# Moving the exps of two chunks ahead of copies, and eight score columns from TensorE to VectorE, in the last head of a streaming attention kernel

## Chip, cores, metric

One core of a Trainium2 chip. The metric is the device time of one execution in microseconds (us), here the median of several executions; a profile was taken of one execution in each run of a kernel. Engines in the profile: PE = TensorE (PEld its weight loads), DVE = VectorE, ACT = ScalarE, POOL = GpSimd, SP = SyncE, which issues the loads.

## The reference

One decode step of a pre-norm transformer block. What matters here is the attention over a long cache:

```python
q = (layernorm(x) @ wq) split into 32 heads of 192          # one query row
scores = einsum("bhqd,bhkd->bhqk", q, k_cache) * 192 ** -0.5   # 32768 keys a head
p = softmax(scores)
o = einsum("bhqk,bhkd->bhqd", p, v_cache)
h = x + o @ wo
out = h + relu(layernorm(h) @ w1) @ w2                       # feed-forward, 640 -> 1536 -> 640
```

Both caches together are 805 MB of bfloat16, each byte used once.

## The kernel before

The kernel streams heads through SBUF. Each head is cut into chunks of 32 columns of 128 keys. For part of a chunk's columns (`jp`), PE transposes the keys into PSUM, ScalarE copies them out, PE multiplies by the query, and ScalarE takes the exp (`exp_pe`). For the other `jd = jc - jp` columns VectorE does a multiply and a reduction, and ScalarE takes that exp too (`exp_dve`). Then PE multiplies all columns by the values. The last head has its own table of chunks, ten of them, the last four small:

```python
JPS = (20, 16)                      # PE columns of even and odd chunks
ends = [(c // 2, (c % 2) * J, J, JPS[c % 2]) for c in range(NC - 2)]      # NC = 8, J = 32
ends += [(NL - 1, 0, 20, 12), (NL - 1, 20, 20, 12), (NL, 0, 16, 8), (NL + 1, 0, 8, 8)]
```

ScalarE's program in a head (engines run in program order; waits are on semaphores):

```python
for c in range(n):
    ...
    copies(g, h, c)                 # waits for the transposes of chunk c
    if h == LAST:
        if c > 5:
            exp_dve(g, h, c - 2)    # waits for VectorE's scores
        if c > 0:
            exp_pe(g, h, c - 1)     # waits for PE's scores
        if 0 < c < 5:
            exp_dve(g, h, c - 1)
if h == LAST:
    exp_dve(g, h, n - 2)
exp_pe(g, h, n - 1)
exp_dve(g, h, n - 1)
```

PE's program in the last head, its beginning and its end. All PE scores go to one PSUM tile, so the scores of chunk c wait for the exp of chunk c - 1:

```python
transposes(g, h, 0)
transposes(g, h, 1)
scores_pe(g, h, 0)
values(g, h, 0)             # waits for both exps of chunk 0
scores_pe(g, h, 1)
transposes(g, h, 2)
o_turn(g, h - 1)            # turns the output of the head before; VectorE waits for it
values(g, h, 1)
...
scores_pe(g, h, 8)
scores_pe(g, h, 9)
for c in (5, 6, 7):
    values(g, h, c)
den_mm(g, h)                # sum of the softmax denominators
values(g, h, 8)
values(g, h, 9)
```

The softmax here doesn't subtract the row's maximum and nothing guards it: scores larger than these inputs give would overflow.

## Time and profile before

| | value |
|---|---|
| time, three runs before the prediction | 1922.64 us median (1921.29 to 1923.37) |
| span of the profiled execution | 1923.4 us |
| time, 38 runs of this kernel in the whole study | 1923.2 us mean (1920.7 to 1925.8) |

The prediction shows the page and the chain. Besides those, from the page, the busy time of each engine:

```profile
PE 1557.5 (81%) x15908; PEld 1087.0 (57%) x15908; DVE 1560.1 (81%) x732; ACT 938.8 (49%) x2000; POOL 1.0 (0%) x6
```

PE and VectorE are equally busy. Two lines of the timeline of the last head (start, duration, engine, line, operation, and in brackets the idle time before it with what ended it):

```profile
1872.23 0.22 DVE L723 TENSOR_SCALAR oT<-mm,odd 128x3 bf16<-128x3 f32 x1 [1.37 <-PE mm L364]
1903.46 0.45 PE L364 MATMUL sp<-qm,kT 128*128 128x2 bf16 x12 [0.36 <-ACT pB L613]
```

The first: VectorE waits 1.37 us for PE's turned output. The second is the scores of chunk 9, from which PE runs without a gap to its last value product.

### The profile page before, as it was taken

The page shows a single profiled execution, that of the slowest core. Times are in us where ns is not written, and L with a number is a line of the kernel's source. Part 1 is how long each engine was busy: PE and PEld are TensorE (multiplying, and loading weights), DVE is VectorE, ACT ScalarE, POOL GpSimd, SP SyncE. Part 2 cuts the span into 40 slices and gives each one's busy share as a digit, 9 for nine tenths or more (in the row PEclk, how much of TensorE's full clock was granted, in tenths as well). Part 3 has the DMA queues.
Part 4 walks back from the last instruction along what each step waited for, and adds up shares of the span by engine and source line. Part 5 has one row for each costly group of instructions (what it writes and reads, how often), then busy time and mean ns, then how long its engine had stood idle before and what let it go on. Part 6 is the DMA issues. An engine that isn't in the chain of part 4 may idle for free.

```text
span 1923.4 us, 36133 instructions
## 1 busy us (share of the span) xinstructions
PE 1557.5 (81%) x15908; PEld 1087.0 (57%) x15908; DVE 1560.1 (81%) x732; ACT 938.8 (49%) x2000; POOL 1.0 (0%) x6
## 2 busy tenths in 40 slices
PE   7878887887888788878878877878787878788788
PEld 7555555655565555555655555555555556555555
DVE  2797787987878978789887879878798787897886
ACT  2455454554544554545544535545455445455444
POOL 0000000000000000000000000000000000000000
PEclk9788998888988889988899888899888898888888
DMA  9999999999999999999999999999999999999997
GB/s 411 423 437 430 429 436 431 438 427 436 433 438 427 436 433 430 439 430 433 437 429 431 440 427 437 435 430 436 433 430 433 439 427 437 430 434 437 430 430 300
DMA packets 29634, 825.29 MB, mean 429 GB/s; under 512 B 3115, under 2 KB 4652, under 8 KB 8108
## 3 DMA queue, kind: packets, MB, share of 16 engines
q1 hardware_dynamic: 29610, 824.98, 99.5%
q8 instruction: 15, 0.25, 0.0%
q14 instruction: 7, 0.06, 0.0%
q10 hardware_dynamic: 2, 0.00, 0.0%
HBM read 824.97 MB, written 0.00 MB: 429 GB/s over the span
## 4 chain that ended last, share of the span: by engine, by line
DVE 39%; DMA 38%; PE 16%; ACT 6%; issue 1%; DVEq 0%; POOLq 0%; SPq 0%
DMA kt<-in_A_k_cache_dram 34%; DVE sc L701 18%; DVE pr L698 18%; PE o_ps L364 8%; PE tp L383 6%; ACT kT L607 5%; DMA va<-in_A_v_cache_dram 4%; PE sp L364 1%; DVE o_pair L713 1%; ACT pA L622 1%; DVE oT L723 0%; DMA kt<-in_A_wq_dram 0%; DVE rec L706 0%; DVE rec L707 0%; DVE odd L719 0%
## 5 line engine op out<-in xcount | busy, mean ns | idle before, releaser
L698 DVE TENSOR_TENSOR pr<-kt,qb 128x2304 f32<-128x2304 bf16 (+2 forms) x257 | 755.9, 2941 | 316.1 <-POOLq L325 288.1
L607 ACT COPY kT<-tp 128x1024 bf16<-128x1024 bf16 (+1 forms) x899 | 814.4, 1016 | 286.8 <-PE tp L383 286.8
L383 PE MATMUL tp<-ident_f,kt 128*128 128x128 f32 x3459 | 588.5, 330 | 238.4 <-POOLq L346 160.9
L701 DVE TENSOR_REDUCE sc<-pr 128x12 f32<-128x2304 f32 (+2 forms) x257 | 755.3, 2939 | 8.9
L383 PEld LDWEIGHTS tp<-ident_f,kt 128*128 128x128 f32 x3459 | 482.5, 170 | 290.4 <-POOLq L346 166.2
L364 PE MATMUL o_ps<-va,pB 128*2 128x384 bf16 x1152 | 222.6, 341 | 62.7 <-POOLq L346 62.7
L364 PEld LDWEIGHTS sp<-qm,kT 128*128 128x128 bf16 x6918 | 197.7, 98 | 83.4 <-issue 43.4
L364 PE MATMUL o_ps<-vb,pB 128*2 128x384 bf16 x1154 | 217.4, 335 | 27.2 <-ACT pA L622 25.0
L364 PE MATMUL sp<-qm,kT 128*128 128x2 bf16 x6918 | 214.7, 164 | 25.7 <-ACT pB L613 24.5
L622 ACT ACTIVATE pA<-sc 128x12 bf16<-128x12 f32 (+2 forms) x257 | 58.3, 227 | 338.8 <-DVEq L65 338.8
L613 ACT ACTIVATE pB<-sp 128x20 bf16<-128x20 f32 (+2 forms) x258 | 52.1, 202 | 307.2 <-PE sp L364 307.2
L364 PEld LDWEIGHTS o_ps<-va,pB 128*2 128x2 bf16 x1152 | 94.3, 86 | 159.2 <-POOLq L346 70.2
L364 PE MATMUL o_ps<-va,pA 128*2 128x384 bf16 x896 | 172.8, 334 | 0.0
L364 PE MATMUL o_ps<-vb,pA 128*2 128x384 bf16 x894 | 167.7, 328 | 0.0
L364 PEld LDWEIGHTS o_ps<-vb,pB 128*2 128x2 bf16 x1154 | 90.9, 85 | 129.1 <-ACT pA L622 30.8
L364 PEld LDWEIGHTS o_ps<-va,pA 128*2 128x2 bf16 x896 | 77.6, 87 | 76.9 <-issue 10.8
L364 PEld LDWEIGHTS o_ps<-vb,pA 128*2 128x2 bf16 x894 | 75.5, 84 | 71.3 <-issue 1.9
L613 ACT ACTIVATION_READ_ACCUMULATOR pB<-sp 128x1 f32 x258 | 55.1, 213 | 0.0
L622 ACT ACTIVATION_READ_ACCUMULATOR pA<-sc 128x1 f32 x257 | 53.1, 207 | 0.0
L364 PE MATMUL o_ps<-xn_ln,kt 128*96 128x1 bf16 (+1 forms) x316 | 22.3, 208 | 2.6 <-DMA kt<-in_A_wq_dram 2.6
L364 PEld LDWEIGHTS o_ps<-xn_ln,kt 128*96 128x96 bf16 (+1 forms) x316 | 22.2, 176 | 2.6 <-issue 2.6
L713 DVE TENSOR_SCALAR o_pair<-o_ps,rec 2x384 bf16<-2x384 f32 x32 | 19.4, 605 | 2.8 <-PE o_ps L364 1.7
(69 smaller groups left out, 187.3 us busy)
## 6 DMA issues: line engine op xcount, KB each, us to landing
kt<-in_A_k_cache_dram SPq DMA_DIRECT2D x62, 6144.0 KB, 26.8
vb<-in_A_v_cache_dram SPq DMA_DIRECT2D x63, 3072.0 KB, 20.8
va<-in_A_v_cache_dram SPq DMA_DIRECT2D x31, 6144.0 KB, 26.8
kt<-in_A_k_cache_dram SPq DMA_DIRECT2D x3, 3072.0 KB, 21.0
wo_s<-in_A_wo_dram SPq DMA_DIRECT2D x16, 480.0 KB, 19.0
kt<-in_A_wq_dram SPq DMA_DIRECT2D x4, 1536.0 KB, 10.8
va<-in_A_v_cache_dram SPq DMA_DIRECT2D x1, 3072.0 KB, 23.1
va<-in_A_v_cache_dram SPq DMA_DIRECT2D x2, 1536.0 KB, 33.9
```

Source lines behind the costliest of these rows:

```text
L364: return lambda: pe.matmul(o, lhsT=w, rhs=r, **kw)
L383: calls.append(lambda b=b, o=o: pe.transpose(out=dst[:, b, :], in_=src[:, o:o + 2 * P].bitcast(f32), identity=ident_f[:]))
L607: g.do(lambda: act.copy(out=kT[c % 2][:, b0:b0 + nb, :], in_=src[:, 0:nb, :].bitcast(bf16)), "act_pe", ("cp", h, c, k))
L613: g.do(lambda: act.activation(out=pB[c % NB][:, 0:jp], in_=sp[:, 0:jp], func=F.Exp, scale=SCALE, accum_out=dsums[:, 2 * c + 1:2 * c + 2]), ...
L622: g.do(lambda: act.activation(out=pA[c % NB][:, 0:jd], in_=sc[c % NC][:, 0:jd], func=F.Exp, scale=SCALE, accum_out=dsums[:, 2 * c:2 * c + ...
L698: g.chain(lambda: dve.tensor_tensor(out=pr[:, 0:j1 - j0, :], in0=src[:, (off + j0) * Dh:(off + j1) * Dh].rearrange("p (j d) -> p j d", d=D ...
L701: g.chain(lambda: dve.reduce_sum(out=sc[c % NC][:, j0:j1], in_=pr[:, 0:j1 - j0, :], axis=X), "dve")
L713: g.do(lambda: dve.tensor_scalar_mul(out=o_pair[:, :, 1, :], in0=o_ps[0:2, 0:2 * Dh].rearrange("q (i d) -> q i d", i=2), scalar1=rec[0:2, ...
```

## The change

The intent: chunk 0's and chunk 1's exps come straight behind their scores, so that PE need not wait for them through the next chunk's copies; chunks 0 and 2 give VectorE 16 columns instead of 12, which spares PE and ScalarE work.

```diff
-    ends = [(c // 2, (c % 2) * J, J, JPS[c % 2]) for c in range(NC - 2)]
+    ends = [(c // 2, (c % 2) * J, J, JPS[c % 2] if c > 3 else 16) for c in range(NC - 2)]
@@ ScalarE, last head
                 if c > 5:
                     exp_dve(g, h, c - 2)
-                if c > 0:
+                if c > 2:
                     exp_pe(g, h, c - 1)
-                if 0 < c < 5:
+                if c < 2:
+                    exp_pe(g, h, c)
+                    exp_dve(g, h, c)
+                elif 2 < c < 5:
                     exp_dve(g, h, c - 1)
```

## The prediction

> **What bounds the kernel now.** I read the page first, then the chain of waits of the last head in order of time, then the last 70 us engine by engine, then stretches of 5 us for the clock and the DMA.
>
> ```profile
> DMA  9999999999999999999999999999999999999997
> q1 hardware_dynamic: 29610, 824.98, 99.5%
> ```
>
> The DMA row (mean busy share of the 16 DMA engines, in 40 slices) and the queue's share say that the kernel streams its caches for the whole span; no change to the last head touches the first 31. Only what lies between the end of the stream and the end of the program can be won. Two stretches (the columns after the widths are busy time of PE, PEld, DVE, ACT, POOL; then clock, DMA share, GB/s) show where the stream ends:
>
> ```profile
> 1905.00:1910.00 5.00, 5.00 (x32) 2.55 (x30) 0.00 (x0) 0.52 (x1) 0.00 (x0) 1.00 1.00 373
> 1910.00:1915.00 5.00, 3.71 (x38) 2.33 (x38) 1.60 (x10) 0.00 (x0) 0.00 (x0) 0.93 0.08 29
> ```
>
> It ends near 1911 us, and the span is 1923.4 us. The chain in the last head (start, duration, what):
>
> ```profile
> 1861.12 0.90 PE sp L364 x30
> 1862.02 2.24 issue
> 1864.26 5.28 PE o_ps L364 x16
> 1869.54 0.72 PE sp L364 x24
> 1870.26 0.51 PE tp L383 x4
> 1870.77 0.02 issue
> 1870.79 3.55 ACT kT L607 x4
> 1874.34 0.17 ACT pB L613 x2
> 1874.51 0.20 ACT pA L622 x2
> 1874.71 0.04 issue
> 1874.75 2.76 PE o_ps L364 x16
> ...
> 1903.46 0.45 PE sp L364 x12
> 1903.91 5.94 PE o_ps L364 x36
> ```
>
> sp are scores, tp transposes, o_ps the products with the values, kT the copies out of PSUM. From 1874.75 on, PE has hardly a gap until its last value product at 1912.2, so the end is PE's backlog, and the backlog begins in the two holes at the top: PE idle 2.24 us before chunk 0's values (the "issue" is really the wait for both exps of chunk 0), which then run cold in 5.28 us instead of 2.76 as for chunk 1; then 2.56 us idle (1872.20 to 1874.75) before chunk 1's values. Why the exps are late, in ScalarE's order of time:
>
> ```profile
> 1857.51 6.30 ACT L607 COPY kT<-tp 128x1024 bf16<-128x1024 bf16 x7 [7.54 <-PE tp L383]
> 1863.63 0.27 ACT L613 ACTIVATE pB<-sp 128x20 bf16<-128x20 f32 x1
> 1870.79 3.55 ACT L607 COPY kT<-tp 128x1024 bf16<-128x1024 bf16 x4 [6.63 <-PE tp L383]
> 1874.19 0.23 ACT L613 ACTIVATE pB<-sp 128x16 bf16<-128x16 f32 x1
> ```
>
> Chunk 0's scores are done at 1862.0, but its exp stands behind the copies of chunk 1 as well (7 copies of 0.90 us). Chunk 1's scores are done at 1870.3, but its exp stands behind chunk 2's copies. Beside this VectorE runs without a gap from chunk 3 to chunk 8 (three lines of it):
>
> ```profile
> 1872.65 3.36 DVE L698 TENSOR_TENSOR pr<-kt,qb 128x3072 f32<-128x3072 bf16 x1
> 1897.21 1.75 DVE L701 TENSOR_REDUCE sc<-pr 128x8 f32<-128x1536 f32 x1
> 1900.97 1.75 DVE L701 TENSOR_REDUCE sc<-pr 128x8 f32<-128x1536 f32 x1
> ```
>
> The second is the end of chunk 7 (1898.96), the third of chunk 8 (1902.72). They will matter below.
>
> **What the Trainium skill says.** "TensorE: Matmul & The Clock Gate", Part 1: the array drops to half its clock after about a 3.4 us window without enough activity and needs such a window of work to come back. The trace agrees: the granted clock is 0.51 from 1865 to 1870, and value matmuls begin there at 336 ns instead of 179. "Perfetto Trace Analysis", Tensor Engine Instruction: ScalarE and VectorE are strict FIFO; so an exp that is ready cannot pass a copy that waits, as seen above. "VectorE: DVE Perf Modes", the TRN2 errata section, gives (N+151)/0.96 ns for a 1x tensor_tensor: 3.357 us for 3072, 2.557 for 2304; the trace has 3.36 and 2.56. "ScalarE: Activation LUTs", What ACT_TABLE_LOAD costs, gives 186 ns + 0.833 ns per element for an immediate-operand ACTIVATE, about 0.2 us for 16 columns; the trace has 0.18 to 0.28.
>
> **The change part by part.**
>
> Columns. Chunks 0 and 2 go from 20 PE columns and 12 on VectorE to 16 and 16. VectorE: per chunk (3.36 - 2.56) + (3.35 - 2.55) = 1.6 us more. PE: per chunk 3 transposes (12 take 1.53 us, 15 take 1.83: 0.3 us) and 6 score matmuls (0.90 to 0.75) less. ScalarE: one copy of 0.8 to 0.9 us less. Value products: 16 matmuls as before.
>
> VectorE's first 1.6 us are mostly hidden. Chunk 0 starts at 1850.86 when its keys land and now ends at 1857.60, told at about 1857.7; PE's denominator is ready at 1857.04, where VectorE waited 1.03 us. So chunk 1 is 0.68 us late, 1858.66, and ends at 1865.38. Chunk 2's keys land at 1865.3 to 1865.4 (issue 1837.57 plus 27.7 us), so it starts at 1865.5, only 0.1 late, ends at 1872.24 instead of 1870.56; the turned output of the previous head, for which VectorE waited 1.37 us until 1872.23, is by then ready. Chunk 3 starts at about 1873.03 instead of 1872.65. Of 3.2 us added, 0.4 remain.
>
> Order. Chunk 0: three copies end at 1857.51 + 2.7 = 1860.2; scores 1860.25 to 1861.0; exps 1861.05 and 1861.23 (VectorE's scores lie ready); values start at about 1861.6 instead of 1864.26, and with about 0.8 us of idle before them I expect them warm: to 1864.4 instead of 1869.5. Copies of chunk 1 run beside them, 1861.45 to 1864.2; its scores 1864.4 to 1865.1, its exps 1865.15 and 1865.5 (after VectorE's 1865.38). Transposes of chunk 2 from 1865.4, when the keys land, to 1867.0; the turn 0.3; values of chunk 1 at about 1867.2 instead of 1874.75: **7.5 us earlier at this point**.
>
> What remains of it downstream, step by step: values of chunk 2 wait for a load that lands at 1879.8 (1856.70 + 23.1): 1879.9 instead of 1886.6, gain 6.7, after a long low stretch, so probably cold, which the slack bears. The second exp of chunk 3 now waits for VectorE (1873.03 + 6.7 = 1879.8). Transposes of chunk 6 wait for keys that land at 1884.4 (1857.07 + 27.3) or for PE: about 1885 instead of 1891.6. The second exp of chunk 5 waits for VectorE, 1891.95; scores of chunk 7 at about 1892.6 instead of 1898.7, gain 6.1. The second exp of chunk 7 stands ahead of the first of chunk 8 and waits for VectorE's chunk 7: 1898.96 + 0.38 = 1899.34, exp 1899.45, first exp of chunk 8 0.20 later, scores of chunk 9 another 0.32 later (both gaps as before: 1903.14 to 1903.46), 1899.95 instead of 1903.46. **Gain 3.5 us**: VectorE has become the limit. Behind it the order is unchanged: values of chunks 5 to 7, denominator, chunks 8 and 9. Their loads land by 1902, VectorE's chunk 8 by 1903.1, all before PE asks. The value loads are released earlier, but the queue was never dry, so they and the weights land as before: first weights at about 1906.6 (used at 1911.7), the last near 1911 (used at 1913.8 instead of 1917.32). So the 3.5 us reach the end: 1922.64 - 3.5 = 1919.1.
>
> **The rivals.**
> 1. The gain of 6 to 7 us survives to the end (1916). For it: PE has no gap from 1874.75 to the end. Against: VectorE's row, which cannot be passed: chunk 7 ends at 1898.96 with no gap behind it.
> 2. PE, now waiting about 2.7 us before the scores of chunk 9, goes cold just before its 8.4 us of last value products; one window at half clock costs about 3.4/2 = 1.7 us, so 1920.8. For it: 5.2 us between value products with 2.8 us of idle mostly left them cold in earlier heads (1842.38: 318 ns). Against: of some twenty such stretches of 3.3 to 4.8 us, only two were cold; here it is 3.6 us. I give it 1 in 5.
> 3. The stream bounds the end and nothing is won (1922.6). For it: DMA is at 9 tenths to the last slice. Against: it ends near 1911, six us before the product that needs its last bytes starts.
> 4. The added VectorE columns and the in-order exps stall ScalarE so long that the new order loses, up to 1924. Against: its copies gain 5 us before the first such wait that did not exist before.
>
> **Range and chances.** The centre is 1919.2: 3.5 us of gain, with a little taken off for rival 2. Before ranges over 2.1 us in three runs, and my chain may be off by 1 us either way: 1917.3 to 1921.6. Two per cent are 38 us, out of reach when only the last 60 us change: faster 0.003, within 0.994, slower 0.003.
>
> **What would show it right or wrong.** First values of the last head at about 10.8 us after the keys of chunk 0 land (13.4 before), at 180 ns each; values of chunk 1 7.5 us earlier; VectorE's chunk 3 about 0.4 us later; a new hole in PE before the scores of chunk 9, ended by ScalarE's exp, which itself waited for VectorE; DMA's end unmoved near 1911. The step most likely to fail is the last: if PE has no hole there, it was PE and not VectorE that set the end; if the hole is there and the products after it take over 300 ns, it is rival 2. It is wrong altogether if the stream ends at another time, or an earlier head differs.

## The result, and the profile after

| | before | after |
|---|---|---|
| timed on the same chip, 4 runs each | 1922.83 us (1921.29 to 1923.37) | 1922.93 us (1920.84 to 1923.39) |
| ratio of means | | 1.000, 95% interval 0.9982 to 1.0017 |
| span of the profiled execution | 1923.4 us | 1920.8 us |

All ratios here are the mean time of one kernel's runs over that of the other's of the same rounds, so not quite the ratio of the medians quoted. No gain of 3.5 us is seen, and the time lies outside the predicted range. The traces differ by 2.6 us in span all the same (0.6 us of it because the last head began earlier), so I read where the predicted gain appeared and where it went. PE in the changed kernel's last head:

```profile
1861.15 1.46 PE L364 MATMUL o_ps<-vb,pB 128*2 128x384 bf16 x8 [0.61 <-issue]
...
1899.43 0.45 PE L364 MATMUL sp<-qm,kT 128*128 128x2 bf16 x12 [1.29 <-ACT pB L613]
1899.81 2.17 PE L364 MATMUL o_ps<-va,pB 128*2 128x384 bf16 x8
1901.77 2.48 PE L364 MATMUL o_ps<-va,pA 128*2 128x384 bf16 x8
```

The first part worked as intended: the values of chunk 0 start at 1861.15 (1864.26 before) and run warm, at 182 ns each (a value product is called warm here at about 180 ns, with a granted clock of 1.00, and cold at 300 ns and more, with a clock near 0.5); those of chunk 1 start at 1866.45 (1874.75). The last three lines are the new hole: PE waits 1.29 us for ScalarE's exp before the scores of chunk 9, and chunk 5's value products behind it are cold (2.48 us for 8, where 8 take 1.46 warm). The hole is shorter than the 2.7 us of the prediction because chunk 4's value products ahead of it were cold too (16 in 4.4 us, where warm ones take 2.8); where they were warm, in the second trace (run 2 below), it is 2.98 us. The chain of waits shows who set the hole:

```profile
1895.28 1.77 DVE pr L701
...
1897.07 1.76 DVE sc L704
...
1898.92 0.30 ACT pA L622 x2
1899.22 0.16 ACT pB L613 x2
...
1899.43 0.45 PE sp L364 x12
1899.88 7.62 PE o_ps L364 x36
```

The chain now runs through VectorE's chunk 7 (pr, sc), its exp (pA), the exp of chunk 8 behind it in ScalarE's order (pB), and the scores of chunk 9 (sp). The 36 value products of chunks 5 to 7 take 7.62 us in the chain; the same 36 took 5.94 us before. VectorE ahead of this:

```profile
1868.33 3.35 DVE L704 TENSOR_REDUCE sc<-pr 128x16 f32<-128x3072 f32 x1
...
1872.10 0.22 DVE L726 TENSOR_SCALAR oT<-mm,odd 128x3 bf16<-128x3 f32 x1
...
1872.51 3.36 DVE L701 TENSOR_TENSOR pr<-kt,qb 128x3072 f32<-128x3072 bf16 x1
```

It waits for nothing between chunk 2 and chunk 3 any more: the wait of 1.37 us for the turned output is gone, and a longer chunk 2 stands in its place. Clock and stream (columns as in the prediction):

```profile
1900.00:1905.00 5.00, 5.00 (x22) 2.20 (x21) 2.56 (x2) 1.74 (x5) 0.00 (x0) 0.66 1.03 413
1910.00:1915.00 5.00, 3.45 (x98) 3.11 (x99) 1.84 (x11) 0.56 (x2) 0.00 (x0) 0.91 0.05 17
```

The granted clock is 0.66 of full speed where it was 1.00 before; the stream ends before 1911 as it did.

To compare traces whose last head begins at different times I count from VectorE's first instruction of the last head, which starts when its first keys land. The table is worked out from the timelines; "scores 9" is the start of PE's scores of chunk 9, "to den" the time from there to the denominator's matmul, "head" the time to the end of the span.

| trace | start | VectorE chunk 3 | scores 9 | to den | head |
|---|---|---|---|---|---|
| before, 1st | 1850.86 | 21.79 | 52.60 | 6.32 | 72.54 |
| before, 2nd | 1850.67 | 20.53 | 52.02 | 6.33 | 71.63 |
| before, 3rd | 1850.28 | 20.59 | 49.33 | 6.33 | 69.02 |
| before, 4th | 1849.89 | 20.54 | 52.21 | 6.32 | 72.21 |
| after, 1st | 1850.23 | 22.28 | 49.20 | 8.00 | 70.57 |
| after, 2nd | 1849.87 | 22.28 | 49.20 | 8.00 | 70.53 |
| after, 3rd | 1851.88 | 22.28 | 49.19 | 6.33 | 68.82 |
| order only | 1850.77 | 20.53 | 47.68 | 6.33 | 67.33 |
| columns only | 1849.94 | 22.28 | 49.77 | 6.32 | 69.46 |
| order, 16 columns in chunk 0 | 1850.17 | 20.68 | 47.60 | 6.32 | 67.23 |
| order, 16 columns in chunk 2 | 1850.59 | 22.15 | 49.40 | 6.32 | 69.11 |
| after + idle matmuls | 1850.05 | 22.28 | 49.20 | 6.32 | 69.05 |
| after + values 5 moved | 1850.92 | 22.28 | 50.27 | 3.72 | 67.48 |
| best parts | 1851.62 | 20.69 | 48.17 | 3.72 | 65.78 |

The table hides one difference ahead of the last head. PE's denominator of the head before starts 5.74 us after "start" in the first trace of the kernel before and 4.06 to 4.10 us in its other three; in the changed kernel's three it is 5.75, 4.06 and 4.06. Where it is late, a group of 16 value products of the head before (at 1842.38 in the first trace) had run cold, in 4.4 us instead of 2.8. So both first traces begin the last head with PE 1.7 us behind.

(In the two last rows with moved values, chunk 5's value products stand ahead of the scores of chunk 9, so "to den" holds only those of chunks 6 and 7.)

### The profile page after: what moved, and what is told of

Same layout as the page of the kernel before. It is cut to its first block, busy times and chain, and to the rows that moved or that the text cites. A ratio compares the mean times of both kernels' runs of the same rounds, so it can differ in the third digit from the quotient of the medians.

```text
span 1920.8 us, 36095 instructions
## 1 busy us (share of the span) xinstructions
PE 1558.5 (81%) x15890; PEld 1090.5 (57%) x15890; DVE 1563.3 (81%) x732; ACT 938.0 (49%) x1998; POOL 1.0 (0%) x6
## 4 chain that ended last, share of the span: by engine, by line
DVE 42%; DMA 37%; PE 14%; ACT 5%; issue 1%; DVEq 0%; POOLq 0%; SPq 0%
DMA kt<-in_A_k_cache_dram 35%; DVE sc L704 20%; DVE pr L701 20%; PE o_ps L364 7%; PE tp L383 6%; ACT kT L607 4%; DMA va<-in_A_v_cache_dram 2%; DVE o_pair L716 1%; PE sp L364 1%; ACT pA L622 0%; DVE oT L726 0%; DMA kt<-in_A_wq_dram 0%; DVE rec L709 0%; DVE rec L710 0%; DVE odd L722 0%
## 5 line engine op out<-in xcount | busy, mean ns | idle before, releaser
L701 DVE TENSOR_TENSOR pr<-kt,qb 128x3072 f32<-128x3072 bf16 (+2 forms) x257 | 757.5, 2948 | 314.9 <-POOLq L325 286.8
L704 DVE TENSOR_REDUCE sc<-pr 128x16 f32<-128x3072 f32 (+2 forms) x257 | 756.9, 2945 | 8.9
L622 ACT ACTIVATE pA<-sc 128x16 bf16<-128x16 f32 (+2 forms) x257 | 58.0, 226 | 349.7 <-DVEq L65 349.7
L613 ACT ACTIVATE pB<-sp 128x16 bf16<-128x16 f32 (+2 forms) x258 | 51.8, 201 | 306.0 <-PE sp L364 306.0
## 6 DMA issues: line engine op xcount, KB each, us to landing
kt<-in_A_wq_dram SPq DMA_DIRECT2D x4, 1536.0 KB, 10.9
```

Of the source, the lines that this page charges most:

```text
L613: g.do(lambda: act.activation(out=pB[c % NB][:, 0:jp], in_=sp[:, 0:jp], func=F.Exp, scale=SCALE, accum_out=dsums[:, 2 * c + 1:2 * c + 2]), ...
L622: g.do(lambda: act.activation(out=pA[c % NB][:, 0:jd], in_=sc[c % NC][:, 0:jd], func=F.Exp, scale=SCALE, accum_out=dsums[:, 2 * c:2 * c + ...
L701: g.chain(lambda: dve.tensor_tensor(out=pr[:, 0:j1 - j0, :], in0=src[:, (off + j0) * Dh:(off + j1) * Dh].rearrange("p (j d) -> p j d", d=D ...
L704: g.chain(lambda: dve.reduce_sum(out=sc[c % NC][:, j0:j1], in_=pr[:, 0:j1 - j0, :], axis=X), "dve")
```

## The experiments

All kernels gave the reference's result, and all timed runs of 1 to 9 are fast runs; runs 10 to 12 are one execution each, which has no state of its own ("unknown" in the record). Three calls of four kernels each; the medians of the kernel before in them were 1923.45, 1924.12 and 1923.52 us, over 9 runs each. The cause first put forward (theory A) was: order frees PE, then VectorE sets the scores of chunk 9, and the clock behind the hole gives back 1.7 us. Rivals: the loads before the last head vary (B); the eight columns eat what the order wins (C).

**1. The kernel before, again** (no edit; 5 runs).

> The kernel before, unchanged, for a second trace and the spread. In its first trace the last head took 72.7 us from the landing of its first keys (1850.7) to the end (1923.4), and that execution (1925.2 us) was slower than all four timed ones (1921.3 to 1923.4). Theory A (the clock's phase: the last head of the kernel before is often shorter than in its first trace, where chunk 0's and chunk 2's values were cold): this trace's last head takes 70.5 to 71.5 us, with chunk 0's value matmuls or chunk 2's at about 180 ns. Theory B (the stream of the heads before varies, the last head does not): the last head takes 72.7 us again and its start is earlier or later. Time ratio 1.000 either way.

Measured: 1922.38 us median (1920.73 to 1924.74), ratio 0.9993 (0.9979 to 1.0006). The last head took 71.6 us, just beyond the upper end of theory A's range, with both named value groups cold again, wholly or in part; its traced execution (1924.10 us) was again slower than the mean. VectorE's chunk 3 started at 20.5 us, without the 1.37 us wait of the first trace. Neither theory is settled by it; it does show that the first trace was not typical in that wait: PE came to the last head 1.7 us later there (see under the table).

**2. The changed kernel, again** (no edit; 5 runs).

> The changed kernel, unchanged. In its first trace the last head took 70.7 us from 1850.1 to 1920.8, with chunk 5's value matmuls cold (16 of them in 4.4 us instead of 2.8) behind a hole of 1.29 us. Theory A: 69.0 to 70.8 us, 1.7 us less where those matmuls are warm. The scores of chunk 9 follow VectorE's chunk 7 by 0.6 us in any case. Time against before: 1.000 plus or minus 0.0008.

Measured: 1922.36 us median (1922.28 to 1922.55), ratio 0.9994 (0.998 to 1.0008). Scores of chunk 9 at 49.20 us, to the hundredth as before, and cold behind the hole again. Chunk 0's value products were cold too this time, after only 0.60 us of idle.

**3. Order only.**

```diff
-... JPS[c % 2] if c > 3 else 16) for c in range(NC - 2)]
+... JPS[c % 2]) for c in range(NC - 2)]
```

> The new places of the exps, with 12 columns on VectorE for chunks 0 and 2 as before. Theory A (VectorE sets the scores of chunk 9): VectorE's chunk 7 ends 0.4 us earlier, so the time is 0 to 0.5 us below the changed kernel's. Rival C (the columns eat what the order wins): at least 2 us below the changed kernel, 0.999 of before or less.

Measured: 1919.86 us median (1918.70 to 1921.10), ratio 0.9981 (0.9967 to 0.9994): 2.5 us below the changed kernel. Theory A's number for it fell and rival C's was met. VectorE and PE in its trace:

```profile
1865.33 2.56 DVE L701 TENSOR_TENSOR pr<-kt,qb 128x2304 f32<-128x2304 bf16 x1 [1.60 <-POOLq L325]
1871.30 3.36 DVE L701 TENSOR_TENSOR pr<-kt,qb 128x3072 f32<-128x3072 bf16 x1
1898.45 0.45 PE L364 MATMUL sp<-qm,kT 128*128 128x2 bf16 x12 [0.36 <-ACT pB L613]
1898.83 1.46 PE L364 MATMUL o_ps<-va,pB 128*2 128x384 bf16 x8
```

VectorE waits 1.60 us for chunk 2's keys (first line), starts chunk 3 at 20.53 us instead of 22.28, and PE's hole before the scores of chunk 9 is 0.36 us, with warm products behind it. So the columns cost VectorE 1.75 us by chunk 3, where the prediction had counted 0.4 from the first trace of the kernel before. The theory for the runs that follow: chunk 0's extra columns lie in VectorE's wait for keys and are free, chunk 2's are what costs (tested by 7 and 8); the clock's part is tested by 4 and 5.

**4. The values of chunk 5 ahead of the scores of chunk 9, in the changed kernel.**

```diff
         scores_pe(g, h, 8)
+        values(g, h, 5)
         scores_pe(g, h, 9)
-        for c in (5, 6, 7):
+        for c in (6, 7):
             values(g, h, c)
```

> The changed kernel, with the values of chunk 5 in front of the scores of chunk 9, so that PE works in the hole while ScalarE waits for VectorE. Theory A: the hole goes, and PE's last value product ends about 3 us earlier than in the changed kernel's first trace (1906.9 instead of 1909.9, if its last head starts at the same time), so 1.3 to 3 us below the changed kernel, ratio to before about 0.9988. Rival (the stream of loads bounds the end): its last landing near 1911 leaves no gain over 0.5 us.

Measured: 1919.42 us median (1919.14 to 1920.23), ratio 0.9979 (0.9965 to 0.9992), 2.9 us below the changed kernel. The hole is gone; the last value group starts at 55.6 us instead of 58.8. The stream did not bind here.

**5. Twelve idle matmuls in the hole, in the changed kernel.**

```diff
         scores_pe(g, h, 8)
+        for _ in range(12):
+            g.do(mmul(mm[0:2, 208:496], ident_b[:, 0:2], wide[:, 0:288], start=True, stop=True, skip_group_check=True))
         scores_pe(g, h, 9)
```

> The changed kernel with 12 idle matmuls (2x288, constant operands, result never read) in front of the scores of chunk 9, to keep the array's clock up in the hole; no useful work is moved. If the cold clock gives back 1.7 us (rival 2 of the prediction): scores of chunk 9 still 49.2 us after VectorE's start of the last head, but 6.3 us from there to the denominator instead of 8.0, last head 68.9 instead of 70.5 us, time 1.7 us below the changed kernel. If the cold clock does not matter: 70.5 us and the changed kernel's time.

Measured: 1921.17 us median (1920.83 to 1922.25), ratio 0.9986 (0.9973 to 1.0). In the trace:

```profile
1896.19 1.63 PE L364 MATMUL mm<-wide 128*2 128x288 bf16 x12
1899.25 0.45 PE L364 MATMUL sp<-qm,kT 128*128 128x2 bf16 x12 [1.42 <-ACT pB L615]
1899.63 1.46 PE L364 MATMUL o_ps<-va,pB 128*2 128x384 bf16 x8
```

Scores of chunk 9 at 49.20 us as predicted, warm products behind, 6.32 us to the denominator, head 69.05 us. The size of the clock's loss is thus measured: 8.00 against 6.32, 1.7 us. But the changed kernel's third trace (run 12) was warm without the idle matmuls, so one warm trace does not show that they caused it, and the two ratios' intervals overlap. What is shown is the loss when it is cold.

**6. Columns only.**

```diff
-    ends = [(c // 2, (c % 2) * J, J, JPS[c % 2]) for c in range(NC - 2)]
+    ends = [(c // 2, (c % 2) * J, J, JPS[c % 2] if c > 3 else 16) for c in range(NC - 2)]
```

> 16 columns on VectorE for chunks 0 and 2, exps in their old places. Theory (columns load VectorE with 1.6 us, order frees PE): values of chunk 1 start about 1 us earlier than in the kernel before, since a copy, six transposes and twelve score matmuls are gone, PE stays the limit, and the last head takes 70.5 to 71.8 us: 0.5 to 1.5 us below the kernel before. Rival (the columns alone are harmful): at or above the kernel before.

Measured: 1921.24 us median (1920.74 to 1923.29), ratio 0.9988 (0.9974 to 1.0001), so perhaps below the kernel before, not clear of noise. In the trace the scores of chunk 9 stand at 49.77 us with a hole of 0.36 us, the head at 69.46 us, below the 70.5 to 71.8 us expected; but chunk 2's values were warm here, and a head of the kernel before with those warm takes 69.02 us. Chunk 1's values start 21.4 us after the head's start, against 21.3 to 23.9 us in the four traces of the kernel before, so the 1 us earlier that was expected is not shown. The columns alone are not harmful; they also gain nothing that I could show.

**7. Order, with 16 columns for chunk 0 only.**

```diff
-JPS[c % 2] if c > 3 else 16)
+16 if c == 0 else JPS[c % 2])
```

> The new order with 16 columns for chunk 0 only. VectorE waits 1.6 us for chunk 2's keys in the order-only run, so chunk 0's extra 1.6 us should be hidden there: chunk 3 starts on VectorE 20.5 to 20.8 us after the head's start, scores of chunk 9 at 47.6 to 48.0 us, time within 0.4 us of the order-only run. If it is not hidden: 22 us, 49 us, and 2 us or more above.

Measured: 1919.72 us median (1919.07 to 1920.61), ratio 0.9978 (0.9965 to 0.9992). Chunk 3 on VectorE at 20.68 us and scores of chunk 9 at 47.60: both as expected.

**8. Order, with 16 columns for chunk 2 only.**

```diff
-JPS[c % 2] if c > 3 else 16)
+16 if c == 2 else JPS[c % 2])
```

> The new order with 16 columns for chunk 2 only. Nothing hides chunk 2's extra 1.6 us on VectorE: chunk 3 starts there at 22.1 us after the head's start, scores of chunk 9 at 49.1 us behind a hole of over 1 us, the values after them cold, time equal to the changed kernel's within 0.5 us and 2 to 2.5 us above the run with chunk 0 only. If the loss came from chunk 0: the time of the order-only run.

Measured: 1922.44 us median (1921.47 to 1923.34), ratio 0.9993 (0.9979 to 1.0006): the changed kernel's ratio, and 2.7 us above run 7 on the same chip. Chunk 3 on VectorE at 22.15 us, scores of chunk 9 at 49.40. I had expected a hole of over 1 us with cold products; in the trace PE was late itself (chunk 4's values were the cold ones), the hole was 0.36 us and the products after it warm. VectorE's first line of chunk 3 in run 7, from its timeline:

```profile
1870.85 3.36 DVE L701 TENSOR_TENSOR pr<-kt,qb 128x3072 f32<-128x3072 bf16 x1
```

and chunks 2 and 3 in run 8:

```profile
1865.16 3.36 DVE L701 TENSOR_TENSOR pr<-kt,qb 128x3072 f32<-128x3072 bf16 x1 [1.61 <-POOLq L325]
1872.74 3.36 DVE L701 TENSOR_TENSOR pr<-kt,qb 128x3072 f32<-128x3072 bf16 x1
```

In run 8 VectorE idles 1.61 us before chunk 2, for keys that have not landed, and then carries a longer chunk 2 on to the end. In run 7 the longer chunk 0 fills that idle time. Of the two times four columns, those of chunk 0 are free and those of chunk 2 cost their full 1.6 us.

**9. The best parts together**: the order, 16 columns for chunk 0 only (as in 7), and chunk 5's values moved (as in 4).

> The best parts together: the new order, 16 columns for chunk 0 only, and the values of chunk 5 in front of the scores of chunk 9. In the run with chunk 0 only, PE still had a hole of 1.24 us before those scores, so PE should be done with the values 1.2 us earlier. If nothing else binds, the last head takes 66.0 instead of 67.2 us and the time is 1.2 us below that run's. If the stream binds (its last bytes land near 1911.4, and the second feed-forward product started at 1911.3 in that run), the second feed-forward product waits for its weights and the gain is 0 to 0.4 us.

Measured: 1918.66 us median (1917.51 to 1919.27), ratio 0.9974 (0.9961 to 0.9988): 4.9 us in the mean below the kernel before (1918.43 against 1923.37), the lowest of all, though its interval overlaps those of runs 3, 4 and 7. Head 65.8 us, near the 66.0 expected if nothing else binds. In the 60 matmuls of its second feed-forward product, from 1910.89 us, a gap of 0.20 us stands before the last 15, which none of the other thirteen traces has. This product takes its weights in pieces as they land, and the stream ran until about 1912 in this trace, so I take it that the stream begins to bind here; I did not test it.

**10 and 11. The kernel before, a third and a fourth trace** (no edit; 1 run each).

> The kernel before, for a third trace. Two traces gave last heads of 72.5 and 71.6 us, both from executions slower than the timed mean of 1923.2. If the spread of the timed runs comes from which value products of the last head the array takes cold: this last head lies between 70.0 and 72.6 us, and its difference to 72.5 us is made up by value groups that are warm here. If it comes from the heads before: 71.6 to 72.6 us whatever the time.

> The kernel before, for a fourth trace, with the same two readings as for the third: 70.0 to 72.6 us in the last head by its cold groups, or 71.6 to 72.6 us whatever the time.

Measured: 1921.18 and 1923.87 us; last heads 69.0 and 72.2 us. In the third trace chunk 2's values, from PE's timeline:

```profile
1884.43 1.79 PE L364 MATMUL o_ps<-va,pB 128*2 128x384 bf16 x10
1886.05 1.14 PE L364 MATMUL o_ps<-va,pA 128*2 128x384 bf16 x6
```

They are warm, 2.8 us in all; in the other three traces they took 4.4 to 4.8 us, for instance 10 in 3.03 us at 1886.59 in the first. So 1.7 to 2.0 us of the 2.6 to 3.5 us between the third trace and the others is this one group, and it is not made up later: by the scores of chunk 5, right behind the group, the first trace lies 3.27 us behind the third, and by those of chunk 9 still 3.27 us. In the first trace the other 1.6 us were there before the group, with PE's late start. The third head, 69.0 us, lies below the 70.0 to 72.6 us expected by 1 us, so the range was too narrow; the reading by cold groups stands, and the other reading (71.6 us or more whatever the time) is refuted. The fourth head fits both.

**12. The changed kernel, a third trace** (no edit; 1 run).

> The changed kernel, for a third trace. Scores of chunk 9 at 49.2 us after VectorE's start of the last head, as in both others. Chunk 5 to 7's values: 8.0 us to the denominator if cold again (last head 70.5 us), 6.3 us if warm (68.9 us). Cold in all three would say that the hole brings the cold window nearly always, not 1 time in 5.

Measured: 1922.61 us; scores of chunk 9 at 49.19 us, warm behind the hole, head 68.8 us. So cold in two of three traces, neither nearly always nor rarely. Its time is no better for it, because its last head began late, at 1851.9 us.

## Why the prediction was wrong

The step that failed is the last one, "So the 3.5 us reach the end: 1922.64 - 3.5 = 1919.1". The path up to the scores of chunk 9 held. Two terms of the sum were mis-sized: the gain at that point, 3.4 us against the one trace but 2.34 us against four, and the cold products behind the new hole, charged with 0.1 us and costing 1.1 us on average.

*Placing the order's gain.* Right. Chunk 0's values were to start at 10.8 us after the head's start and came at 10.9 in the first trace. That it agrees so closely is partly luck, since both first traces have PE 1.7 us late; in the two others it is 9.2 us. They ran warm, 182 ns each, in two of three traces. Chunk 1's values were to come 7.5 us earlier and came 7.7 earlier (23.89 to 16.22 us after the head's start). Scores of chunk 9 were to be 3.5 us earlier than in the trace of before and were 3.4 us earlier (52.60 to 49.20). The new hole, ended by an exp that waited for VectorE, was there in every trace of the changed kernel. The stream's end did not move.

*"Of 3.2 us added, 0.4 remain."* Against the trace that it was read from, it held: chunk 3 came at 22.28 us instead of 21.79, 0.49 later. As a price of the columns it fails, and it is the step with most to learn from. In that trace VectorE lost 1.37 us to a wait that the new order removes anyway, and that none of the three later traces of the kernel before has, where PE came on time (chunk 3 starts at 20.5 to 20.6 us there). So the columns took up the time that the order had just freed. Runs 3, 7 and 8 measure it: by chunk 3 the columns cost 1.75 us, all of it chunk 2's; at the scores of chunk 9, where VectorE sets the pace, 1.5 us (47.68 to 49.20); in the time, with the hole that they open, 2.5 us.

*Rival 2, the cold array, "1 in 5".* Mis-sized. It came in two of three traces and cost 1.68 us each time. The estimate of the loss, 1.7 us, was right; the chance was read from some twenty stretches of the earlier heads and did not carry over: here the array went cold after 2.1 us between value products with 1.29 us of idle (first trace), and after 3.8 us with 2.98 (second).

*"1922.64 - 3.5 = 1919.1."* The subtraction. The 3.5 us were worked out from a trace whose execution took 1925.23 us, and taken from a median of 1922.64. Over the four traces of the kernel before, the scores of chunk 9 come at 51.54 us on average, not 52.60: in this kernel a cold group costs its full time (run 10), and some executions are spared it. In the changed kernel they come at 49.20 in all three, since VectorE sets them. The sum in the means is thus 51.54 - 49.20 = 2.34 us, less the cold products (8.00, 8.00 and 6.33 against 6.33: 1.11 us on average), 1.2 us up to the denominator; the heads differ by 1.38 us (71.35 to 69.97). In the time, the kernel before averages 1923.2 us (38 runs) and the changed one 1922.5 us (10 runs): 0.7 us, which the intervals of the two direct comparisons (1.000 and 0.9994, both including 1) do not separate from nothing.

*The other rivals.* Rival 1 (6 to 7 us survive) is refuted by the scores of chunk 9 at 49.2 us. Rival 3 (the stream bounds the end) is refuted for this change by runs 3 and 4, which are faster. Rival 4 (slower) did not come about, though its mechanism, exps that stall ScalarE for VectorE, is what makes the hole.

*Smaller readings of the prediction.* "PE has no gap from 1874.75 to the end" is not so: PE waits 0.97 us before the scores of chunk 7 (at 1898.70), besides gaps of 0.2 to 0.4 us. And "the trace agrees" with the skill's window only in part: the half clock is there, but by stretches of a quarter of a us it begins at about 1863.1, 1.1 us after PE's last score product, so no whole window of idle time lies ahead of it.

*Open.* The last head begins between 1849.9 and 1851.9 us in these traces. That offset is as large as the effects sought and partly hid them; what sets it was not tested. Timed runs leave no trace, so how often each cold group comes is known only from three and four traces. The heads differ by 1.4 us in the traces and the times by only 0.7 us. Of that, 0.2 us is a later start of the head in the changed kernel's traces (1850.66 against 1850.43 on average), and 0.4 us is that the four traced executions of the kernel before are slower than the average of its 38 timed runs (1923.6 against 1923.2 us).

## What to carry to other kernels

When two engines are equally busy, price each part of a change in the schedule that the other parts leave behind: here the order freed the time that the columns then used up, and each part alone did at least as well as both (0.9981 and 0.9988 of the kernel before, against 0.9994 and 1.000; the intervals overlap). Move work only into idle time that stays idle (chunk 0's columns, in the wait for keys), and when a new hole opens before an in-order wait, fill it with work that is ready anyway. A gain that is read off one trace has to be set against the time of that same execution, and where a clock state comes and goes, against several traces.

## What the Trainium skill lacked or had wrong

- "TensorE: Matmul & The Clock Gate", Part 1, names at least one idle window of about 3.4 us as what takes the clock to half, and its table in "Why this matters for your kernels" asks for no gaps over about 3 us. In the changed kernel's first trace the clock fell to half at about 1900.4 us; the longest gap in the 3.4 us ahead of that is the 1.29 us before the scores of chunk 9, with score and value products on both sides of it; in three other traces (runs 5, 7 and 12; in run 5 behind the idle matmuls) gaps of 1.24 to 1.48 us at this place passed warm. In run 7 the clock fell at about 1859.9 us, and the longest gap in the 3.4 us ahead was 0.61 us. So a much shorter gap can do it, and the gap alone does not decide. The page also tells of a kernel whose short idles made the clock swing, but gives no length for them and no rule for windows that are partly busy.
- The same page, Part 1, puts the penalty of the ramp at under 1% of a typical kernel and advises against fitting a count of cold matmuls. It is small here too (1.7 us in 1923), but that is more than the 1.4 us by which the change shortened the traced heads, and in the kernel before one cold value group (4.4 to 4.8 us against 2.8) makes up 1.7 to 2.0 us of a 2.6 to 3.5 us difference between traced executions.
- "VectorE: DVE Perf Modes" gives no measured time for a long `tensor_reduce`, only that it runs at 1x (and a general row for all of VectorE's operations). The runs show 3.35 us for 3072 elements, 2.55 for 2304 and 1.75 for 1536: the same as the `tensor_tensor` beside it, bfloat16 in and float32 out (3.36, 2.56, 1.76), so that a score column costs VectorE twice 0.2 us.
